# Block sums of batch 0's values from the groups fetched for attention, constants written on chip, and a new order of instructions

## The chip, the cores and the metric

The kernel runs on one core of a Trainium2 chip, in one launch. The metric is the device time of one execution in microseconds (us). The core has five instruction streams that run side by side and wait for each other through semaphores: PE (TensorE, matmuls and transposes), ACT (ScalarE), DVE (VectorE), POOL (GpSimd) and SP (SyncE, which here issues all DMAs). Each stream executes its own instructions strictly in order.

## What is computed

Attention with a local window and block summaries feeds a layer that mixes tokens and channels. B = 4 batches, H = 8 heads, S = 768 tokens, D = 64.

```python
k_sum = k.reshape(B, H, nb, 32, D).max(axis=3)        # nb = 24 blocks
v_sum = v.reshape(B, H, nb, 32, D).mean(axis=3)
scores_l = scale * q @ k.T, kept where |pos_q - pos_k| < 16, else -1e9
scores_s = scale * q @ k_sum.T + log(32)
a = softmax(concat([scores_l, scores_s]))
x = a @ concat([v, v_sum])                             # (B, S, 512)
theta = x @ w_theta;  zr, zi = x * cos(theta), x * sin(theta)
y = w_tok_r @ zr + w_tok_i @ zi                        # over tokens
u = x + y
out = u + relu(u @ w_ch)
```

The four weight matrices arrive as 64-bit floats and are turned into 32-bit ones on chip, by integer operations on ACT, POOL and DVE.

## The kernel before

A batch's 768 queries are cut into six tiles of 128, numbered 0 to 23 over the four batches. A tile's 128 rows are two groups of 64 queries, and a group sees 94 local keys (64 and a halo of 15 on either side) beside the 24 block summaries: 118 columns (`NK`), the summaries first. Group j's 96 rows of local values (94, padded to `VL` = 96) come by one DMA from the array `vg` into rows 24 to 119 of a tile `v`; the 24 summed rows are copied into rows 0 to 23. Four such tiles are in rotation.

The steps, with the letters used below and the line of their main instruction:

- **S** scores, 32 matmul records a tile (L465; the first tile's in two halves); softmax of eight heads on DVE (L501) and ACT (L505)
- **P** transposes of the softmax, two halves of four (L514), each copied out of PSUM by ACT or DVE (L518)
- **A** products with the values, 32 records (L488), then the normalisation (L526 to L535)
- **X** transposes of the normalised tile (L544), copied out by ACT or DVE (L294)
- **T** theta, four products over the channels (L569 for tiles 0 to 5, with unsplit 32-bit operands; L574 after that), then the phase (L583 to L587) and cosine and sine (L592 to L599)
- **M** the mix over tokens, per batch, half of the channels and token tile s (L637; the steps of batch 0's first half with unsplit operands)
- at the end, the channel product (L753)

Ahead of a batch stands `prepass`. It loads the keys `kn` (four DMAs of 399 KB for batch 0), takes the block maxima on DVE (L392), and forms the block sums of the values. For batch 0 these sums are matmuls (L398): six token tiles of 128 rows are loaded from `vn` by three DMAs into a tile that later holds `x`, and each is multiplied by a 128 by 24 matrix of zeros and ones (`member`), all six into one PSUM bank. ACT scales the result (`vs`, L421), and copies of it go into the `v` tiles (L443). For the other batches DVE sums tiles from `vT`.

Three constant arrays come from the array `cst`: the zeros and ones (22 KB), three masks of 128 by 118 (177 KB), and the identity used by the transposes (64 KB).

The program is first recorded as a list of steps (`op`), numbered as they are made. A string `ORDER`, found beforehand by a search on a planner's costs, names them in the sequence in which they are issued; a letter behind a number picks the engine (p, a, d, g for PE, ACT, DVE, POOL), else it is the one with the least planned cost. Each engine thus gets its instructions in the order of that string. The planner's costs (`SWITCH`, `c_dve` and so on) act on the kernel only through the string and that choice. One more rule stands in the last loop: where a POOL step and the DVE step just ahead of it in the string are both marked with `BOTH`, the POOL step waits for the DVE step.

Before the scores PE runs five products on zeros (L331), which have no result that is used.

Of the kernel before, what the change touches and what calls it, by code (L numbers as in the profile page):

```python
# [14 lines left out]
ALU = mybir.AluOpType  # L15
# [3 lines left out]
B, H, S, D = 4, 8, 768, 64  # L19
P = 128  # L20
NT = S // P
# [9 lines left out]
NK = NB + NL  # L31
VL = 96
# [23 lines left out]
12 6d 14 0 13 15 4 7 8 28 18 9 10 11 3 16 20 1 22 19 33a 37g 35a 34a 39 38a 17 36a 40 41 49 5 52 56 42 44 43 46 50 54 47 74  # L56
75a 24 2 68 76d 51 45 53 48 55 170a 169a 21 23 25 26 59 57 164 29 31 27d 77 78 79 69d 70d 32d 71 72 30a 171 80 212 86 165
167 215g 216g 168g 58a 60a 172 175 176 179 173 174 178 81a 177 61 180 183 182 181 217 62a 184 187 185 186 65d 63 66 64d 67d
82g 166g 83 73 84 87a 188 190 199 88g 92 93 266 189a 191a 218 219 220 221 200a 192 224 223 270a 222 225 196a 193a 103a 213
214 94 95 89 85 90 226 91 194 227 197 229 230 228 195d 198d 231 233 232 269g 104g 108a 105 106 201 202 203 204 205 206d 207  # L60
234 236 271 245 235a 237a 109g 272 275 110 274 323a 276 279 246a 238 111 280 281 208a 242a 239a 278 285 284 320 268 322 267
96 389 97 98 321 99 100 101 102 107 112 113 114a 119a 282 240 273 283 243 241d 244d 277 287 286 247 248 249 250 251 115g
324g 116 117 252d 253 120g 209 288 325 290 299 300a 301 302 254a 289a 291a 292 326 118 255 121 210 122 211 123 258 303 256
124a 334 336 328 337 327 129a 293a 294 392a 296d 335 329 330 393g 125g 130g 259 304 332 295d 297 341 339 333 338 340 305 331
298a 260 394 342 344 126 131 127 132 128 133 312 134a 139a 343a 306d 307 308a 353 354a 309 345a 395 261 355 313 356 346 357
314 358 135g 140d 136 141 137 142 138 143 144a 149a 310 257 145d 347a 350a 150d 351 151 146 348 349a 352a 147 152 148 153
359 154a 159a 681a 360d 361 403 315 366 368 422 369 155g 160d 156 157 161 158 162 163 362a 423a 363 424 425 426 427 311 262a
# [187 lines left out]
def c_dma(nbytes, run=2048):  # L255
# [700 lines left out]
```

## Time and profile before

| | us |
|---|---|
| median of 3 runs | 454.60 |
| lowest, highest | 454.58, 455.56 |
| the profiled execution's time | 454.5 |
| its span (first to last instruction) | 452.7 |
| PE busy | 440.9 |
| DVE, ACT, POOL busy | 336.2, 271.9, 94.0 |
| moved by DMA | 55.80 MB |

The profile is of one execution. Busy times are the union of an engine's instructions; a matmul's end is modelled, so a stretch of back-to-back matmuls is read best from one start to the next. "Idle before" gives the wait just ahead of an instruction and the instruction that released it. Rows of a timeline merge like instructions that follow each other ("x8").

### The profile page before, as it was taken

The page shows a single profiled execution, that of the slowest core. Times are in us where ns is not written, and L with a number is a line of the kernel's source. Part 1 is how long each engine was busy: PE and PEld are TensorE (multiplying, and loading weights), DVE is VectorE, ACT ScalarE, POOL GpSimd, SP SyncE. Part 2 cuts the span into 40 slices and gives each one's busy share as a digit, 9 for nine tenths or more (in the row PEclk, how much of TensorE's full clock was granted, in tenths as well). Part 3 has the DMA queues.
Part 4 walks back from the last instruction along what each step waited for, and adds up shares of the span by engine and source line. Part 5 has one row for each costly group of instructions (what it writes and reads, how often), then busy time and mean ns, then how long its engine had stood idle before and what let it go on. Part 6 is the DMA issues. An engine that isn't in the chain of part 4 may idle for free.

```text
span 452.7 us, 9375 instructions
## 1 busy us (share of the span) xinstructions
PE 440.9 (97%) x3562; PEld 357.3 (79%) x3562; DVE 336.2 (74%) x930; ACT 271.9 (60%) x595; POOL 94.0 (21%) x98
## 2 busy tenths in 40 slices
PE   8888999999999999999999999999999999999997
PEld 3464655757888888888888888888888878999996
DVE  4799999778576576776638757575654599998996
ACT  2899988887774676966373755366664406526240
POOL 0221204635520103041011100012003100313521
PEclk9999999999999999999999999999999999999999
DMA  8999945323077340412710503101003720000256
GB/s 300 344 332 327 373 154 184 119 60 110 1 227 250 101 119 25 130 42 52 229 37 3 163 1 118 41 3 55 0 2 108 274 85 0 0 19 20 88 186 250
DMA packets 25005, 55.80 MB, mean 123 GB/s; under 512 B 2944, under 2 KB 8320, under 8 KB 24960
## 3 DMA queue, kind: packets, MB, share of 16 engines
q1 hardware_dynamic: 24960, 55.20, 37.4%
q8 instruction: 28, 0.46, 0.4%
q14 instruction: 17, 0.14, 0.1%
HBM read 45.75 MB, written 9.44 MB: 122 GB/s over the span
## 4 chain that ended last, share of the span: by engine, by line
PE 88%; DMA 8%; ACT 2%; DVE 1%; SPq 0%; issue 0%; ACTq 0%
PE m L637 46%; PE t L574 11%; PE c L753 6%; PE m L753 6%; PE pa L488 5%; PE s L465 4%; PE pa L514 4%; PE t L569 3%; DMA wt<-wti 3%; PE t L544 3%; DMA v<-vg 2%; DMA x<-vn 2%; DMA kn<-kT 1%; PE t L753 1%; ACT L598 1%; ACT w L598 0%
## 5 line engine op out<-in xcount | busy, mean ns | idle before, releaser
L637 PE MATMUL m<-wt,zh 128*128 128x512 f32 (+1 forms) x768 | 181.2, 360 | 0.8 <-DVE x L656 0.6
L637 PEld LDWEIGHTS m<-wt,zh 128*128 128x128 f32 x768 | 122.8, 189 | 32.8 <-issue 14.3
L637 PE MATMUL m<-wt,zl 128*128 128x512 f32 x336 | 86.6, 339 | 0.0
L505 ACT ACTIVATE e<-e,st 128x118 f32<-128x118 f32 x192 | 62.9, 388 | 16.3 <-DVE st L501 15.9
L637 PEld LDWEIGHTS m<-wt,zl 128*128 128x128 f32 x336 | 51.2, 188 | 7.4
L501 DVE CUSTOM_DVE_ANT_0 e<-s,cs 128x118 f32<-128x118 f32 x192 | 45.4, 273 | 10.7 <-PE s L465 6.8
L574 PE MATMUL t<-wth,xh 128*128 128x512 f32 x144 | 47.6, 412 | 0.0
L583 ACT ACTIVATE w<-t,bmagic 128x512 f32<-128x512 f32 x24 | 16.5, 688 | 42.2 <-PE t L574 41.3
L448 POOL COPY k<-kn 128x376 f32<-128x376 f32 (+1 forms) x24 | 12.7, 536 | 96.2 <-DVE zl L303 39.8
L488 PEld LDWEIGHTS pa<-v,e 118*64 118x64 f32 x768 | 24.7, 137 | 6.8 <-issue 4.2
L514 PEld LDWEIGHTS pa<-cs,e 128*118 128x118 f32 x192 | 22.7, 136 | 8.9 <-ACT e L505 1.6
L514 PE MATMUL pa<-cs,e 128*118 128x128 f32 x192 | 28.5, 274 | 0.8 <-ACT e L505 0.4
L488 PE MATMUL pa<-v,e 118*64 118x65 f32 x768 | 28.2, 224 | 0.8 <-ACT e L518 0.8
L574 PE MATMUL t<-wth,xl 128*128 128x512 f32 x72 | 28.3, 394 | 0.0
L465 PE MATMUL s<-k,q 64*64 64x118 f32 x768 | 25.3, 268 | 1.3 <-DVE st L527 0.7
L465 PEld LDWEIGHTS s<-k,q 64*64 64x64 f32 x768 | 19.7, 132 | 7.8 <-issue 5.9
L656 DVE TENSOR_TENSOR x<-m,x 128x512 f32<-128x512 f32 (+1 forms) x32 | 16.6, 548 | 11.6 <-PE m L637 11.6
L586 DVE TENSOR_SCALAR w<-w 128x512 f32<-128x512 f32 x19 | 8.6, 451 | 22.4 <-ACT w L583 22.3
L518 DVE COPY e<-pa 118x512 f32<-118x512 f32 x15 | 10.3, 688 | 18.9 <-PE pa L514 18.9
L574 PEld LDWEIGHTS t<-wth,xh 128*128 128x128 f32 x144 | 22.1, 189 | 2.7 <-DVE xl L550 0.3
L303 POOL TENSOR_TENSOR zl<-zb,zh 128x512 fp32r<-128x512 f32 x9 | 11.5, 1289 | 58.6 <-ACT zh L294 31.6
L587 DVE CUSTOM_DVE_ANT_0 w<-t,w 128x512 f32<-128x512 f32 x24 | 16.6, 690 | 8.0 <-POOL w L586 7.4
(168 smaller groups left out, 798.9 us busy)
## 6 DMA issues: line engine op xcount, KB each, us to landing
v<-vg SPq DMA_DIRECT2D x48, 195.0 KB, 4.5
q<-qg SPq DMA_DIRECT2D x24, 256.0 KB, 4.5
kn<-kT SPq DMA_DIRECT2D x6, 798.0 KB, 7.7
wt<-wtr SPq DMA_DIRECT2D x6, 768.0 KB, 10.1
wt<-wti SPq DMA_DIRECT2D x6, 768.0 KB, 11.9
f<-vT SPq DMA_DIRECT2D x12, 384.0 KB, 4.9
cu<-u_scratch SPq DMA_DIRECT2D x8, 384.0 KB, 6.4
out<-cu SPq DMA_DIRECT2D x16, 192.0 KB, 2.5
```

The lines of the kernel that those rows point to most:

```text
L465: mm(0.79 * len(pairs) / NP, [lambda p=p, g=g, h=h: nc.tensor.matmul(sc[h].get()[ROW[g], p], q.get()[ROW[h], p, ROW[g]], k.get()[ROW[h], p ...
L488: mm(2 * 0.433 + scores[0] + (0.2 if scores[0] else 0.0), [lambda n=n, g=g, a=a: nc.tensor.matmul(xa[a].get()[ROW[g], n], turned[a].get()[ ...
L501: op({"DVE": 0.205}, lambda eng, n=n: nc.vector.tensor_tensor_reduce(e()[:, n], sc[n % 2].get()[:, 2 * a + n // 2], mask(m), -SCALE, 3.0e3 ...
L505: op({"ACT": 0.288}, lambda eng, n=n: nc.scalar.activation(e()[:, n], e()[:, n], AF.Exp, bias=st.get()[:, n:n + 1], scale=-1.0), [(st, n)] ...
L514: mm(NH * 0.109, [lambda n=n: nc.tensor.transpose(tp.get()[:NK, n], e()[:, n], ident()) for n in range(NH)], [e_ref, (cs, "ident")], [tp], ...
L544: mm(NC * 0.109, [lambda c=c: nc.tensor.transpose(tx.get()[:, c], xn[b, i].get().rearrange("p h d -> p (h d)")[:, c * P:(c + 1) * P], ident())
L574: calls = [lambda t=t, xx=xx, k=k, c=c: nc.tensor.matmul(th.get(), xx.get()[:, c], w_th[c].get()[:, k], start=(c == 0 and t == 0), stop=(c ...
L583: op({"ACT": 0.59}, lambda e: nc.scalar.activation(r(), th.get(), AF.Identity, bias=bmagic.get(), scale=1.0 / TWO_PI), [th, bmagic], [R], due)
L587: op({"DVE": c_dve(DM)}, lambda e: nc.vector._custom_dve(TENSOR_ADD_SAT, out=r(), in0=th.get(), in1=r(), s0=PI_F, s1=-PI_F), [th], [R], due)
L637: nc.tensor.matmul(acc[th](), zz.get()[:, r, cc], w[:, TT[th]], start=(s == 0 and r == 0 and t == 0 and (th == 0 or c == 0)), stop=(s == N ...
L656: op({"DVE": c_dve(nt * P)}, lambda e, u=u, acc=acc: nc.vector.tensor_tensor(u(), acc(), u(), op=ALU.add), [areg] + [(xs, n) for n in rang ...
L753: calls = [lambda k=k, t=t, x=x, y=y: nc.tensor.matmul(to.get(), weights[n][x][0]()[:, k, j * P:(j + 1) * P], operands[n].get()[:, y, k], ...
```

## The change

**Block sums of batch 0.** The three DMAs from `vn` go. The groups 0 to 7 of batch 0 are fetched in `prepass` (eight DMAs of 195 KB from `vg`, which tiles 0 to 3 need anyway), groups 0 to 3 into the four rotating tiles and groups 4 to 7 side by side in the space of an `x` tile (`wide`). A group's 64 queries cover two blocks of 32, so each group is multiplied by a 96 by 24 matrix of zeros and ones that has two columns of ones (`pair`). The last two token tiles still come from `vn`, 256 KB each. Six products become ten, into the same bank. The tiles 0 to 3 then fetch no values of their own, and there are eight copies of the sums into value tiles instead of four for batch 0.

**Rows.** Local keys come first (rows 0 to 95, two of them padding that the mask removes), the 24 summaries last: 120 columns instead of 118.

**Constants.** The three DMAs from `cst` go. 17 instructions write masks, zeros and ones, and the identity: memsets on DVE and POOL, and `affine_select` on POOL.

**Order.** A new string. Counting the steps as the code makes them, it begins so on each engine (W0 to W3 are the four pieces of `w_theta`, W4, W5, ... those of the token weights; before in brackets where it says more):

- SP: groups 4, 0, 1, 2, keys, group 5, keys, group 3, keys, keys, queries of tile 0, group 6, `vn` 4, group 7, W1, `vn` 5, W0, queries, W3, queries, W2, W4, a group, W5. (Before: keys, keys, zeros and ones, queries, keys, keys, `vn` 0-1, masks, `vn` 2-3, W1, `vn` 4-5, identity, W0, queries, group 0, group 1, W2, queries, W3, group, group, W4, W5.)
- PE: four of the products on zeros, six block-sum products, S0, four block-sum products, P0, S1, A0, the fifth product on zeros, S2, P1, X0, A1, T0, S3, P2, X1, A2, T1, P3, S4, A3, X2, T2, M of s = 0 (four), S5. (Before: five on zeros, S0, six block-sum products, P0, S1, A0, S2, P1, X0, A1, T0, P2, S3, X1, A2, T1, half of P3, S4, half of P3, X2, half of T2, A3, M.)
- POOL: twelve of the constants, in the middle of which the masks, then a copy of key maxima, the identity's second step, key copies.
- ACT, from tile 0's last exponential on: `vs`, W0's first step, two copies of the sums, one half of P0, a copy of the sums, W3's first step, tile 1's exponentials, W2's first step, both halves of P1, X0, a copy of the sums, and tile 2's exponentials mixed with the first steps of W4 and W5 and key copies.
- DVE, from tile 0's softmax on: W1 (five steps), one half of P0, W0's third step, a copy of the sums, W0's fourth, tile 1's softmax, tile 0's normalisation, W3, W0's last, W3, three of tile 2's softmax steps, W3's last, W2's three steps and a step of tile 1's normalisation.

Further on the tiles follow each other as before; where two halves of P stood on either side of a T product, they now mostly stand together. Some 200 steps change between DVE, ACT and POOL. ACT switches between its exponential and sine tables 27 times instead of 23.

```diff
-VL = 96
+LW = NL + 2
+NK = LW + NB
...
-    dma(lambda: sums.get().rearrange("p a n -> p (a n)")[:, :2 * NB - BPT], lambda: cst[:, P + 3 * NK:], (2 * NB - BPT) * 512, [], [sums], 1e6)
-    for k, c in (("mask", slice(P, P + 3 * NK)), ("ident", slice(0, P))):
-        dma(lambda c=c: cs.get()[:, c], lambda c=c: cst[:, c], (c.stop - c.start) * 512, [], [(cs, k)], 1e6)
+    def fill(dst, value, n, wr):
+        op({"DVE": c_dve(n, "fast"), "POOL": c_pool(n, False)}, lambda e: V[e].memset(dst(), value), [], [wr], -100.0, port=BOTH)
+
+    def keep(dst, pattern, n, base, step, compare, value, wr):
+        op({"POOL": c_pool(n, False) + 0.1}, lambda e: nc.gpsimd.affine_select(
+            out=dst(), in_=dst(), pattern=pattern, compare_op=compare, fill=value, base=base, channel_multiplier=step), [], [wr], -100.0, port=BOTH)
...
+    for g in range(2):
+        local = lambda g=g: masks(slice(g * QT, (g + 1) * QT), slice(0, LW))
+        keep(local, [[0, 3], [1, LW]], 3 * LW, 0, -1, ALU.is_ge, far, (cs, "mask"))
+        keep(local, [[0, 3], [-1, LW]], 3 * LW, 2 * HALO, 1, ALU.is_ge, far, (cs, "mask"))
...
-                st = Ref(tpool, [P, NT, DM], tag="x", bufs=K["XB"])
-                for t in range(0, NT, 2):
-                    dma(lambda t=t: st.get()[:, t:t + 2], lambda t=t: vn[b, t:t + 2].rearrange("t p d -> p t d"), 2 * P * DM * 4, [], [(st, t)], due)
-                    mm(2 * 0.93, [product(t, lambda t=t: st.get()[:, t]) for t in (t, t + 1)], [(st, t), sums], [pv], due, mode="block")
+                wide = Ref(tpool, [P, NT * DM], tag="x", bufs=K["XB"])
+                tail = Ref(tpool, [P, DM], tag="zb", bufs=K["ZS"])
+                vbuf[b] = [Ref(apool, [NK, H, DV], tag="v", bufs=K["VB"]) for _ in range(K["VB"])]
...
+                for j, (at, key, _) in enumerate(here):
+                    vload[j] = at, key
+                    loc = (key, "loc") if j < K["VB"] else (wide, (j, "loc"))
+                    dma(lambda at=at: at()[:LW], lambda j=j: vg[b, j], H * (LW + 16) * DV * 4, [], [loc], due, 2080, 0.35)
+                    mm(0.93, [lambda at=at, j=j: nc.tensor.matmul(
+                        pv.get()[:NB].rearrange("n p d -> n (p d)"), flags(pair - 2 * j, pair - 2 * j + NB)[:LW], at()[:LW, :, :D],
+                        start=(j == 0), stop=False)], [loc, sums], [pv], due, mode="block")
+                for t, (at, key) in zip((NT - 2, NT - 1), ends):
+                    dma(at, lambda t=t: vn[b, t], P * DM * 4, [], [key], due)
+                    mm(0.93, [product(t, at)], [key, sums], [pv], due, mode="block")
...
+            if b > 0 or j >= 8:
+                dma(lambda at=at: at()[:LW], lambda j=j: vg[b, j], H * (LW + 16) * DV * 4, [], [keys_v[0]], due, 2080, 0.35)
```

## Rows read from the trace of the kernel before

**Rows 1.** The page: busy time by engine, and GB/s in 40 slices of 11.3 us.

```profile
PE 440.9 (97%) x3562; PEld 357.3 (79%) x3562; DVE 336.2 (74%) x930; ACT 271.9 (60%) x595; POOL 94.0 (21%) x98
GB/s 300 344 332 327 373 154 184 119 60 110 1 227 250 101 119 25 130 42 52 229 37 3 163 1 118 41 3 55 0 2 108 274 85 0 0 19 20 88 186 250
```

**Rows 2.** Busy time by stretches of 5 us: PE, PE's weight loads, DVE, ACT, POOL (with instructions), PE clock, DMA share, GB/s.

```profile
15.00:20.00 5.00, 4.91 (x75) 2.94 (x74) 4.58 (x17) 3.89 (x10) 0.92 (x3) 1.00 1.05 326
...
30.00:35.00 5.00, 4.63 (x77) 3.28 (x75) 4.93 (x17) 4.71 (x14) 0.83 (x1) 1.00 0.99 342
...
45.00:50.00 5.00, 5.00 (x14) 2.64 (x15) 4.92 (x24) 4.97 (x13) 2.08 (x3) 1.00 1.01 355
```

**Rows 3.** The chain of work that ended last, in order of time, its first pieces: start us, us, what.

```profile
6.43 8.30 DMA x<-vn
...
23.77 12.59 DMA wt<-wti
...
44.94 1.49 PE m L637 x4
```

**Rows 4.** The timeline of the first 15 us: start us, us, engine, line, operation, out<-in, count, idle before.

```profile
1.46 7.61 PE L331 MATMUL t<-zb 128*128 128x512 f32 x10 [1.46 <-DVE zb L329]
...
6.75 0.34 PEld L331 LDWEIGHTS t<-zb 128*128 128x128 f32 x1 [0.52 <-issue]
...
7.60 0.22 PEld L331 LDWEIGHTS t<-zb 128*128 128x128 f32 x1 [0.52 <-issue]
...
8.05 0.19 PEld L331 LDWEIGHTS t<-zb 128*128 128x128 f32 x1 [0.24 <-issue]
...
8.98 0.34 POOL L448 COPY k<-kn 128x188 f32<-128x188 f32 x1 [8.53 <-DMA kn<-kT]
...
9.01 0.63 PE L465 MATMUL s<-k,q 64*64 64x118 f32 x16
...
10.81 3.61 PE L398 MATMUL pa<-x,vt 128*24 128x512 f32 x8
```

**Rows 5.** The timeline from 16 to 37 us, the same columns.

```profile
16.70 0.59 ACT L421 ACTIVATE vs<-pa 24x512 f32<-24x512 f32 x1 [0.73 <-PE pa L398]
...
17.32 0.62 ACT L443 COPY v<-vs 24x520 f32<-24x520 f32 x1
17.32 0.42 DVE L443 COPY v<-vs 24x520 f32<-24x520 f32 x1
...
18.04 1.07 ACT L518 COPY e<-pa 118x512 f32<-118x512 f32 x2
18.11 0.69 DVE L361 SCALAR_TENSOR_TENSOR xh<-wth,xh 128x512 int32<-128x512 int32 x1
...
18.89 1.28 PE L488 MATMUL pa<-v,e 118*64 118x65 f32 x31
19.04 0.28 DVE L501 CUSTOM_DVE_ANT_0 e<-s,cs 128x118 f32<-128x118 f32 x1 [0.24 <-PE s L465]
...
20.27 0.64 ACT L353 ACTIVATE xh<-wth 128x512 f32<-128x512 f32 x1
...
20.71 0.16 DVE L527 TENSOR_SCALAR st<-pa 128x4 f32<-128x4 f32 x1
...
21.00 0.61 POOL L357 TENSOR_SCALAR xh<-xh 128x512 f32<-128x512 f32 x1 [0.41 <-ACT xh L353]
...
21.59 0.76 DVE L535 TENSOR_TENSOR xn<-pa,st 128x256 f32<-128x256 f32 x2
...
23.24 0.67 ACT L353 ACTIVATE xl<-wth 128x512 f32<-128x512 f32 x1 [0.75 <-DMA wth<-wth]
...
36.45 0.92 ACT L353 ACTIVATE f<-wt 128x768 f32<-128x768 f32 x1 [0.57 <-DMA wt<-wti]
```

**Rows 6.** PE alone from 24 to 45 us, the same columns.

```profile
24.48 1.46 PE L488 MATMUL pa<-v,e 118*64 118x65 f32 x32 [0.82 <-ACT e L518]
...
29.41 1.04 PE L514 MATMUL pa<-cs,e 128*118 128x128 f32 x8
30.37 1.04 PE L465 MATMUL s<-k,q 64*64 64x118 f32 x32
...
41.88 1.12 PE L569 MATMUL t<-xh,x 128*128 128x512 f32 x2 [1.18 <-ACT x L294]
```

**Rows 7.** PE alone from 206 to 213 us, the same columns; the start-to-start times are what is read.

```profile
206.39 0.86 PE L637 MATMUL m<-wt,zh 128*128 128x512 f32 x4
...
207.52 1.04 PE L465 MATMUL s<-k,q 64*64 64x118 f32 x32
208.49 1.16 PE L488 MATMUL pa<-v,e 118*64 118x65 f32 x32
209.57 0.66 PE L544 MATMUL t<-cs,xn 128*128 128x128 f32 x4
209.99 0.95 PE L637 MATMUL m<-wt,zh 128*128 128x512 f32 x4
...
211.12 0.86 PE L637 MATMUL m<-wt,zh 128*128 128x512 f32 x4
...
212.16 0.86 PE L637 MATMUL m<-wt,zh 128*128 128x512 f32 x4
```

**Rows 8.** Groups of instructions by line: what POOL's dearest form costs (busy us, mean ns of one, idle before).

```profile
L303 POOL TENSOR_TENSOR zl<-zb,zh 128x512 fp32r<-128x512 f32 x9 | 11.5, 1289 | 58.6 <-ACT zh L294 31.6
```

More of the change, by code (lines that the diff above doesn't have):

```diff
@@ L133 @@
+1982 1983 2002 2003 2004
 """
@@ new lines, in attn_moe @@
+    fill(lambda: masks(slice(QT, P), slice(HALO + QT, LW))[:, 2], far, HALO + 2, (cs, "mask"))
+    fill(flags, 1.0, 2 * NB - BPT, sums)
+    keep(flags, [[-BLK, 2 * NB - BPT]], 2 * NB - BPT, BLK * (NB - BPT), 1, ALU.is_ge, 0.0, sums)
+    keep(flags, [[BLK, 2 * NB - BPT]], 2 * NB - BPT, BLK - 1 - BLK * (NB - BPT), -1, ALU.is_ge, 0.0, sums)
+    pair, width = 2 * NB - BPT + NB - 2, 2 * NB - 2
+    fill(lambda: flags(2 * NB - BPT, 2 * NB - BPT + width), 0.0, width, sums)
+    fill(lambda: flags(pair, pair + 2), 1.0, 2, sums)
@@ L438, in att_tile @@
         dma(q.get, lambda: qg[b, i], NP * P * 512, [], [q], due)
-        v = [vbuf[b][(2 * i + g) % K["VB"]] for g in range(2)]
+        v = []
         for g in range(2):
-            dma(lambda g=g: v[g].get()[NB:], lambda g=g: vg[b, 2 * i + g], H * (VL + 16) * DV * 4, [], [(v[g], "loc")], due, 2080, 0.35)
-            if 2 * i + g < K["VB"]:
-                op({"POOL": c_pool(H * DV, False), "ACT": c_act(H * DV), "DVE": c_dve(H * DV, "fast")}, lambda e, g=g: (
-                    nc.scalar.copy if e == "ACT" else V[e].tensor_copy)(v[g].get()[:NB], vs.get()), [vs], [(v[g], "sum")], due, port=BOTH)
+            j = 2 * i + g
+            if b == 0 and K["VB"] <= j < 8:
+                (at, (own, n)) = vload[j]
+                keys_v = [(own, (j, "loc")), (own, (j, "sum"))]
+            else:
+                own = vbuf[b][j % K["VB"]]
+                at, keys_v = own.get, [(own, "loc"), (own, "sum")]
+            v.append((at, keys_v))
+            if b > 0 or j >= 8:
+                dma(lambda at=at: at()[:LW], lambda j=j: vg[b, j], H * (LW + 16) * DV * 4, [], [keys_v[0]], due, 2080, 0.35)
+            if j < (K["VB"] if b else 8):
+                op({"POOL": c_pool(H * DV, False), "ACT": c_act(H * DV), "DVE": c_dve(H * DV, "fast")}, lambda e, at=at: (
+                    nc.scalar.copy if e == "ACT" else V[e].tensor_copy)(at()[LW:NK], vs.get()), [vs], [keys_v[1]], due, port=BOTH)
         k = Ref(apool, [P, NP, 2, NK], tag="k", bufs=K["KB"]) if i < K["KB"] else kbuf[b][i % K["KB"]]
@@ L488, in products @@
         mm(2 * 0.433 + scores[0] + (0.2 if scores[0] else 0.0), [lambda n=n, g=g, a=a: nc.tensor.matmul(
[L489 to L490 removed]
+            xa[a].get()[ROW[g], n], turned[a].get()[:NK, n * P + g * QT:n * P + (g + 1) * QT], v[g][0]()[:NK, NH * a + n], start=True, stop=True)
+            for a in range(2) for n in range(NH) for g in range(2)] + scores[1], v[0][1] + v[1][1] + turned + scores[2], xa + scores[3], due, mode="block")
         for a in range(2):
```

225 lines of the change are left out of this document (112 added, 113 removed).

## The prediction

> **What bounds the kernel now.** I read the page first: PE is busy 440.9 of 452.7 us, every other engine has a quarter of the span or more to spare, and DMA is heavy only in the first 60 us (300 to 373 GB/s in the first five slices) [rows 1]. So the end moves by what is added to or taken from PE's own work, and by PE's waits; DMA, DVE and ACT count only where PE waits for them. The stretches of 5 us show where that is: ahead of 45 us PE has gaps (4.63 of 5 us from 30 to 35) while DMA stands at a share of 1 and DVE at 4.6 to 4.9 of 5 us; from 45 us on PE is full [rows 2]. The chain says the same: up to the first mix step at 44.94 it runs mainly through loads (the values from `vn`, a token weight), and after that through PE [rows 3]. The case is therefore decided in the head, up to M of s = 0; a delay there is carried to the end nearly one to one.
>
> **The start, worked out from the order in the diff.** The products on zeros run in passes: the weight loads, each made one pass ahead, start 0.85 us apart up to 7.60 and 0.45 after it, and the one for pass ten starts with pass nine, at 8.05 [rows 4]. That halving is the step of the clock from 1.2 to 2.4 GHz, though the granted clock is written as 1.00 already. Four of the five products stand first in the new order, so eight passes are over at 8.05 and the first block-sum product can start there, where S0 started at 9.01.
>
> A block-sum product takes two passes: eight records in 3.61 us make 0.45 a pass with the last end counted, and 0.86 a product by passes of 0.43, half the cold 0.85 (these eight are four products) [rows 4]. Ten need 8.6 us where six needed 5.2: 3.4 us more on PE, in order. Six of them stand ahead of S0, so S0 cannot start before 8.05 + 5.2 = 13.25.
>
> Is its data there? SP now issues four groups (780 KB) before the first keys and 2,766 KB up to the last ones; before it was 1,874 KB, landed at about 8.9 (the wait of POOL's first copy ends there) [rows 4]. The third pair of `vn` tiles, at 4,099 KB, landed at 14.73 [rows 3], so 2,225 KB took 5.85 us, 380 KB a us. The last keys come at 8.9 + 892/380 = 11.2, their maximum (1 us) and copies (0.3) make it 12.6: hidden behind the six products, just. The last `vn` tile, at 4,436 KB, lands at 15.6, before its product (17.0) needs it. The fetch of 1.3 MB less (four `vn` tiles and the constants) thus moves nothing in the first 18 us; it lets the weights that wait behind come 0.3 to 3 us earlier.
>
> The constants: POOL has twelve of them ahead of the first product, four of 288 elements. At the rate of its copies (0.34 us for 188) they take 0.45 each and the chain ends near 6 us [rows 4]; at that of its dearest form, 1.29 us for 512 [rows 8], near 7.2. Both are before 8.05, so I take no cost; below nothing it cannot go, since nothing waited for POOL there. Before, the mask's DMA held the first softmax step back; now it waits for S0.
>
> So S0 runs from 13.3 to 14.4, the last four block-sum products to 17.85. ACT then works in order: `vs` 0.59, W0's first step 0.64, two copies 0.62 each, a half of P0 0.54 (two took 1.07) [rows 5]: A0 can start at 21.3, where it started at 18.89 [rows 5], 2.4 late. What queues behind it on PE is S2 and P1. On DVE, W0's third step waits for that ACT step and for POOL's 0.61, then come 0.42, 0.42 and 0.69, and tile 1's softmax starts at 21.8 and ends at 23.5; before it was 19.04 to 20.71 [rows 5], 2.8 late. Normalisation (1.45), P1 (25.2 to 25.9), W2's first step and both halves of P1 on ACT (1.7) bring A1 to 27.35, against 24.48 [rows 6]: 2.9 late. T0's third product needs W2, whose last step on DVE stands behind W3, W0 and three softmax steps: 24.95 + 5.1 = 30.1. T0 ends at 32.0; before it ended at 29.41 [rows 6]. The lag there is 2.6 us, and it contains the 3.4 us of products and 1.0 of the earlier start.
>
> **From T0 to the first mix step.** Before, this took from 29.41 to 44.9, of which PE's work (P2, S3, X1, A2, T1, P3, S4, X2, half of T2, A3 by the starts in rows 6) is 11.8 and waits are 3.7. The new order does the other half of T2 (two products of two passes, 0.86 each) first, so the point to compare with is 46.6. With the same waits M starts at 32.0 + 15.5 + 1.7 = 49.2, a lag of 2.6. With the chain carried on (ACT has four weight steps of 0.92, two copies of keys and a table load among the exponentials, DVE ends tile 3's softmax at 41.2, so P3 starts at 42.4 and T2 at 47.1) it is 50.6, a lag of 4.0. With no wait at all it would be 45.5, 1.1 ahead. The lighter DMA speaks for the lower end, since W3 and a token weight were waited for by 0.75 and 0.57 us [rows 5]; DVE's fill of over 90% speaks for the upper [rows 2]. I take 3.0, between the two counts that have waits.
>
> **From there on.** (1) Changes of kind on PE. A mix step takes 1.04 from start to start, 1.13 after transposes, and 1.13 ahead of scores; A, behind scores, takes 1.08 [rows 7]. After the first mix step the old order has 55 changes from transposes to a wide product and 17 from wide products to scores, the new one 31 and 8: 33 times 0.09 is 3.0 less. It has 14 more changes of other kinds (scores or A next to transposes or to wide products), which rows 6 and 7 bound by 0 and 0.25 (P2 ahead of S3 took 0.96, 0.25 over two halves of 0.36); at 0.14, the middle, that is 2.0 more. Sum: 1.0 less, between 3.0 less and 0.5 more. (2) 120 columns: S takes 0.97 [rows 7]; two columns in 118 over 24 tiles are at most 0.4 us, I take 0.3. The transposes and A have as many moving columns as before; DVE's and ACT's two columns lie beside PE. (3) Five tiles now have both halves of P, then S, then A with nothing between, so both copies out of PSUM (0.54 on ACT [rows 5]) must be done within 0.97. The nearest row is A1, which waited 0.82 with only X0 in between [rows 6]. Bounds 0 and 5 times 0.8; I take 0.2, since S is 0.6 longer than X. (4) POOL takes over work and ACT four more table loads; neither is near full after 100 us, and I take nothing. (5) The waits at X6 and at the prepass of batch 1 have the same neighbours in both orders and stay. The tail after the last product is unchanged.
>
> **Sum.** Against the profiled execution: 454.5 + 3.0 - 1.0 + 0.3 + 0.2 = 457.0. The median of the runs is 454.6, 0.1 above that execution, which changes nothing.
>
> **Rivals.** *The load was the bound, faster.* The chain of the old head is DMA throughout [rows 3]. If what I count as waits for ACT and DVE is shadow of late loads, the 1.3 MB shorten the head: with 1.5 us of waits in place of 7.0 (from S0 at 9.0 to the mix at 44.9 PE had 28.9 of work by the same starts), the new head (34.7 us of PE work from 8.05) ends at 44.3 against 46.6, and with the -1.0 and +0.5 the run takes 451.7. It decides at A0: if A0 starts before 19.5, this holds. Against it stands ACT's fixed order ahead of A0, each step with a row. *Lag and savings cancel.* If T0 ends 2 us late and PE's waits up to the mix fall by 1, the lag is about 1.0, the changes of kind give 1.0 back, the columns and P's copies cost 0.5, and the time is 455.0. *The constants are late.* Everything in the head hangs on POOL's chain, which DVE's memset releases at about 1.5 us; from 8.05 on each us that it ends late is a us more. Were the chain twice as long as by the dearer rate, it would end near 12, and the run takes 461. The trace has no `affine_select`; POOL's first copy took its 0.34 us right behind the load that it waited for [rows 4], so I give this little. The Trainium skill, GPSIMD Engine Reference, section Instruction dispatch, says that the first call of a freshly loaded kernel pays some 6 us of code load that the profile shows as no instruction; by that, as an estimate, the chain would end near 12 to 13. No row here shows such a load.
>
> **How the numbers follow.** About 0.3% of the time, 1.4 us, is what a measurement can tell from no change. Chances: the lag as worked out, 457.0, 0.45 (its own spread of some 2 us puts 0.38 of that over +1.4, 0.06 within, 0.01 below); the load as bound, 451.7, 0.28 (0.25 faster, 0.03 within); cancelling, 455.0, 0.22 (0.04, 0.16, 0.02); late constants, 461, 0.05. Faster 0.30, same 0.25, slower 0.45. The range leaves out the late constants and the lower half of the faster case's spread, and takes in the upper lag with some waits of (3): 451.2 to 460. Its ends stand on different signs; the likeliest case alone has 455 to 459.5.
>
> **What would show it.** The first block-sum product at 8.0 to 8.3 with POOL's last constant before it; S0 near 13.3; A0 near 21, behind ACT's copies and not behind a load; T0's end near 32; the first mix step at 49 to 51, with PE full after it; mix steps after transposes fewer by about twenty. What would make the prediction wrong: a first mix step before 47.5 (the waits of the head shrank), POOL's constants ending after 8 us, or PE gaps of over 2 us in sum after 100 us.

## The result, and the profile after

| | before | after |
|---|---|---|
| time, us (median of 11 runs each, same chip) | 455.22 (453.94 to 457.67) | 458.42 (456.68 to 461.12) |
| profiled execution, us | 454.5 | 458.0 |
| its span, us | 452.7 | 456.3 |

The ratio is 1.0073, with a 95% interval of 1.0055 to 1.0091: 3.3 us slower (2.5 to 4.1), where the forecast was 2.5. Nine of the changed kernel's eleven runs had a mean granted clock of 0.998 or more, with a median of 458.20, so the clock is not what separates the two kernels. The page of the changed kernel, to be held against [rows 1]:

```profile
PE 443.8 (97%) x3570; PEld 358.2 (79%) x3570; DVE 336.6 (74%) x935; ACT 275.2 (60%) x579; POOL 108.0 (24%) x128
GB/s 245 378 344 393 329 11 123 140 30 163 2 168 187 121 165 122 59 1 50 246 59 37 177 26 37 100 36 1 1 2 139 215 108 1 1 0 55 52 192 258
```

PE is 2.9 us busier, ACT 3.3, POOL 14. In its first slice of 11.4 us DMA moved 245 GB/s where it had moved 300. The stretches of 5 us from 5 us on (columns as in [rows 2]) show the same, here of the changed kernel:

```profile
5.00:10.00 5.00, 5.00 (x10) 1.55 (x9) 1.29 (x2) 0.28 (x1) 0.36 (x2) 1.00 1.04 287
10.00:15.00 5.00, 5.00 (x43) 1.59 (x40) 2.88 (x7) 2.14 (x5) 1.71 (x6) 1.00 1.06 340
```

and here of the kernel before:

```profile
5.00:10.00 5.00, 4.64 (x23) 1.83 (x21) 2.88 (x5) 1.29 (x5) 0.34 (x1) 1.00 1.01 370
10.00:15.00 5.00, 4.41 (x25) 1.30 (x26) 2.44 (x20) 3.10 (x10) 0.00 (x0) 1.00 1.05 398
```

DMA is full in all four (its share, the last but one number, is 1.01 to 1.06), and in the changed kernel it moves less. PE's timeline, up to the first mix step:

```profile
8.12 3.61 PE L440 MATMUL pa<-v,vt 96*24 96x512 f32 x8
...
13.44 1.05 PE L516 MATMUL s<-k,q 64*64 64x120 f32 x32
...
18.41 1.40 PE L565 MATMUL pa<-cs,e 128*120 128x128 f32 x8
...
21.51 1.15 PE L539 MATMUL pa<-v,e 120*64 120x65 f32 x32 [0.72 <-ACT e L569]
...
31.52 1.05 PE L516 MATMUL s<-k,q 64*64 64x120 f32 x32
...
44.67 1.13 PE L620 MATMUL t<-xh,x 128*128 128x512 f32 x2 [0.68 <-ACT x L295]
...
48.20 2.31 PE L688 MATMUL m<-wt,zh 128*128 128x512 f32 x6
```

The start came as worked out: first block-sum product 8.12 (8.05), S0 13.44 (13.3), A0 21.51 behind an ACT copy (21.3), T0's end 31.52 (32.0). The first mix step stands at 48.20, 1.6 behind the 46.6 that the kernel before is to be compared with, where I took 3.0.

Both are single executions, and the head differs between executions of the same instructions (more on that with the order, below).

To see the rest, I added up for each step of PE the start-to-start time that it takes where nothing waits (mix 1.04, S 0.97, A 1.09, a half of P or X 0.36, a block-sum product 0.86, and so on): 415.6 us before, 419.0 after, and the difference is the four products. What is left over at each point is waits, gaps and changes of kind:

| PE reaches | before, us | left over, us | after, us | left over, us |
|---|---|---|---|---|
| first mix step | 44.88 | 18.1 | 48.20 | 16.2 |
| S of tile 8 | 97.46 | 22.0 | 100.98 | 21.0 |
| S of tile 14 | 182.32 | 25.8 | 187.38 | 23.9 |
| S of tile 18 | 245.81 | 27.9 | 246.97 | 27.7 |
| last product | 448.18 | 33.6 | 451.52 | 33.5 |

Up to the first mix step the changed kernel has 5.16 us more work, 1.72 of it the half of T2 that now stands first, and it gets there 3.32 us later. So the head does save 1.8 us of waits, and all of it is given back later: the end is 3.34 us late, and the four products are 3.44. That equality is a sum, not a cause; the experiments say what is in it. Two places of the give-back, on PE of the changed kernel: the transposes of tile 15 (X15) and a late mix step. The kernel before has no wait at the first, and one of 0.62 at the second (the last row):

```profile
229.33 0.66 PE L595 MATMUL t<-cs,xn 128*128 128x128 f32 x4 [1.21 <-DVE w L638]
...
368.72 0.98 PE L688 MATMUL m<-wt,zh 128*128 128x512 f32 x4 [1.21 <-DVE x L707]
```

```profile
365.56 0.73 PE L637 MATMUL m<-wt,zh 128*128 128x256 f32 x3 [0.62 <-DVE x L656]
```

### The profile page after: what moved, and what is told of

Read it like the earlier page. It is cut to its first block, busy times and chain, and to the rows that moved or that the text cites. A ratio compares the mean times of both kernels' runs of the same rounds, so it can differ in the third digit from the quotient of the medians.

```text
span 456.3 us, 9421 instructions
## 1 busy us (share of the span) xinstructions
PE 443.8 (97%) x3570; PEld 358.2 (79%) x3570; DVE 336.6 (74%) x935; ACT 275.2 (60%) x579; POOL 108.0 (24%) x128
## 4 chain that ended last, share of the span: by engine, by line
PE 77%; issue 7%; ACT 6%; DVE 5%; DMA 3%; POOL 1%; SPq 0%; ACTq 0%; DVEq 0%; POOLq 0%
PE m L688 39%; PE t L625 9%; PE c L804 6%; PE m L804 5%; PE pa L539 4%; PE s L516 4%; PE pa L565 3%; DMA x<-vg 3%; PE t L595 2%; ACT e L556 2%; PE t L620 2%; ACT f L382 1%; DVE wt L393 1%; DVE f L390 1%; PE t L804 1%
## 5 line engine op out<-in xcount | busy, mean ns | idle before, releaser
L556 ACT ACTIVATE e<-e,st 128x120 f32<-128x120 f32 x192 | 62.7, 388 | 13.1 <-DVE st L552 12.7
L552 DVE CUSTOM_DVE_ANT_0 e<-s,cs 128x120 f32<-128x120 f32 x192 | 44.9, 274 | 4.2 <-PE s L516 1.7
L565 PEld LDWEIGHTS pa<-cs,e 128*120 128x120 f32 x192 | 21.8, 137 | 6.6 <-ACT e L556 2.8
L565 PE MATMUL pa<-cs,e 128*120 128x128 f32 x192 | 26.0, 274 | 1.0 <-ACT e L556 0.4
L539 PEld LDWEIGHTS pa<-v,e 120*64 120x64 f32 x704 | 22.3, 137 | 5.2 <-issue 3.0
L539 PE MATMUL pa<-v,e 120*64 120x65 f32 x704 | 25.4, 224 | 0.7 <-ACT e L569 0.7
L516 PE MATMUL s<-k,q 64*64 64x120 f32 x768 | 25.3, 269 | 0.3 <-issue 0.3
L707 DVE TENSOR_TENSOR x<-m,x 128x256 f32<-128x256 f32 (+1 forms) x32 | 16.5, 550 | 10.2 <-PE m L688 10.2
L569 ACT COPY e<-pa 120x512 f32<-120x512 f32 x30 | 17.0, 588 | 10.5 <-PE pa L565 10.4
L295 ACT CAST wt<-cb 128x768 fp32r<-128x768 f32 x15 | 12.3, 841 | 15.7 <-POOL cb L729 9.1
```

The costliest lines, as they stand in the source:

```text
L516: mm(0.79 * len(pairs) / NP, [lambda p=p, g=g, h=h: nc.tensor.matmul(sc[h].get()[ROW[g], p], q.get()[ROW[h], p, ROW[g]], k.get()[ROW[h], p ...
L539: mm(2 * 0.433 + scores[0] + (0.2 if scores[0] else 0.0), [lambda n=n, g=g, a=a: nc.tensor.matmul(xa[a].get()[ROW[g], n], turned[a].get()[ ...
L552: op({"DVE": 0.205}, lambda eng, n=n: nc.vector.tensor_tensor_reduce(e()[:, n], sc[n % 2].get()[:, 2 * a + n // 2], mask(m), -SCALE, 3.0e3 ...
L556: op({"ACT": 0.288}, lambda eng, n=n: nc.scalar.activation(e()[:, n], e()[:, n], AF.Exp, bias=st.get()[:, n:n + 1], scale=-1.0), [(st, n)] ...
L565: mm(NH * 0.109, [lambda n=n: nc.tensor.transpose(tp.get()[:NK, n], e()[:, n], ident()) for n in range(NH)], [e_ref, (cs, "ident")], [tp], ...
L569: lambda e: (nc.scalar.copy if e == "ACT" else nc.vector.tensor_copy)(t.get()[:NK], tp.get()[:NK].rearrange("k n q -> k (n q)")), [tp], [t ...
```

## The experiments

Each ran beside the kernel before on its chip. Differences are ratio less one, times 455.

**The products taken out, by place.** The late ones:

```diff
-                        start=(j == 0), stop=False)], [loc, sums], [pv], due, mode="block")
+                        start=(j == 0), stop=(j == 5))][:j < 6], [loc, sums], [pv], due, mode="block")
...
-                    mm(0.93, [product(t, at)], [key, sums], [pv], due, mode="block")
+                    mm(0.93, [], [key, sums], [pv], due, mode="block")
```

> The changed kernel without the four block-sum products that stand behind S0 (groups 6 and 7, tiles 4 and 5 of vn); their loads stay. The block sums of batch 0 then cover only the first 386 values or so, so the output differs in that part. PE and load theory: these products cost 3.44 us of PE and wait for loads that land at 15.5 and 17.3 us; without them the copy of the block sums starts at about 14.6 instead of 18.4, A0 near 17.7 instead of 21.5, and the run is 3.0 to 3.9 us shorter than the changed kernel, 454.5 to 455.4, the time of the kernel before. Order theory (the new order of the rest costs the 3 us, and PE's first 20 us are slack): under 1 us shorter, about 458. Constants theory: no change, 458.4.

The early ones:

```diff
-                        start=(j == 0), stop=False)], [loc, sums], [pv], due, mode="block")
+                        start=(j == 4), stop=False)][:j > 3], [loc, sums], [pv], due, mode="block")
```

> The changed kernel without the four products of groups 0 to 3, which stand ahead of S0; their loads stay. The block sums then lack the first 256 values or so, and the output differs in that part. PE work alone (each 0.86 us in the in-order queue counts wherever it stands): 3.4 us shorter, 455.0. Loads set the end of the block sums (the last group lands at 15.5, the last tile of vn at 17.3): S0 moves at most to its keys, 12.6, A0 stays within 0.5 us of 21.5, and the time is 457.9 to 458.4. The two together, with the run without the late products, say whether the work or the landing holds the head.

Measured: 1.0053 (1.0024 to 1.0081) without the late ones, 1.0120 (1.0090 to 1.0150) without the early ones: 3.4 us of PE's work gone, and the first kernel is 0.9 faster than the changed one, within its interval, the second 2 slower. Both PE theories fell: the first run came where the order theory had put it, the second is outside both of its expectations. PE of the kernel without the late products, and stretches of it (columns as in [rows 2]):

```profile
14.21 1.05 PE L516 MATMUL s<-k,q 64*64 64x120 f32 x32 [0.39 <-POOL k L499]
18.36 1.69 PE L565 MATMUL pa<-cs,e 128*120 128x128 f32 x8 [3.10 <-ACT e L556]
```

```profile
15.00:20.00 5.00, 1.79 (x20) 0.96 (x11) 3.90 (x22) 3.90 (x11) 0.55 (x2) 0.94 1.03 387
20.00:25.00 5.00, 4.71 (x80) 3.56 (x83) 4.68 (x26) 4.90 (x12) 2.47 (x5) 0.72 0.88 342
```

P0 waits for an exponential until 4.15 us behind S0's start. In the changed kernel that would be 17.6, and its late products end at 18.4: by these rows all but 0.8 of their 3.4 us lie in the shadow of tile 0's softmax. PE, idle for 3.1 us, was granted 0.72 of its clock in the stretch from 20 us (the last but two number). Without the early products PE was busy for 0.60 of the 5 us from 10, and the granted clock was 0.74, 0.50 and 0.73 in the stretches from 10, 15 and 20 us. These two runs thus mix less work with a slower clock. The next one keeps PE busy:

```diff
+                    if j > 5:
+                        mm(0.93, [zeros], [idle], [bank], due, mode="block")
+                        continue
```

> The changed kernel with the four products behind S0 replaced by products on zeros of the same shape into another bank: PE stays as busy, but the copy of the block sums no longer waits for the loads of groups 6 and 7 and of tiles 4 and 5, nor for these products. The block sums lack that part, and the output differs. If that wait sets A0: the copy moves from 18.4 to 14.6 and A0 from 21.5 to between 18.9 and 19.5, the run 2 to 2.6 us shorter, 456. If the softmax of tile 0, behind S0 at 13.4, sets the head (in the run without these products PE waited for an exponential until 18.4): P0 stays at 18.4, A0 moves by under 1 us, and the time is 457.6 to 458.4.

Measured 1.0061 (1.0042 to 1.0080), 2.8 us, 0.5 better than the changed kernel and within the interval. Its PE, at S0 and A0:

```profile
14.55 1.05 PE L521 MATMUL s<-k,q 64*64 64x120 f32 x32 [0.61 <-POOL k L504]
...
22.76 1.15 PE L544 MATMUL pa<-v,e 120*64 120x65 f32 x32 [0.60 <-ACT e L574]
```

The block sums were complete at 14, and S0 started 1.1 later than in the profile of the changed kernel, A0 1.25 later. From S0 to A0 it is 8.2 us, against 8.1 in the changed kernel and in the run without the late products: A0 follows S0 and not the end of the block sums. (This profiled execution took 461.47 against a median of 458.24; its excess lies far behind the head, where PE waited 1.86 us ahead of X15 and the granted clock then fell.) S0 first, then:

```diff
-42 20d 21 22 23 24 34 36 38 26 44 28 40 32 30 56 46 50 48 100 52 94 190 8d 9 0d 15g 1g 2 3 4 5 6g 7g 10 11d 12g 13 14 19 27
+26 28 32 30 56 42 20d 21 22 23 24 34 36 38 44 40 46 50 48 100 52 94 190 8d 9 0d 15g 1g 2 3 4 5 6g 7g 10 11d 12g 13 14 19 16
```

> The changed kernel with the keys and the first queries loaded ahead of the groups, and S0 ahead of all block-sum products, as in the kernel before; the rest in its order. S0 moves from 13.4 to about 9, the block sums end at about 19. If S0's place is what the head pays for (tile 0's softmax behind it): P0 can start at 19 at once and the head is 0.5 to 1.5 us shorter, 456.9 to 457.9. If the ten products set it wherever they stand: A0 stays at 21.3 to 22, and the time is 458.0 to 459.0.

Measured 1.0134 (1.0109 to 1.0160), 6.1 us, outside both expectations. PE of this kernel, and its stretches (columns as in [rows 2]):

```profile
10.00 1.05 PE L515 MATMUL s<-k,q 64*64 64x120 f32 x32 [2.34 <-DMA q<-qg]
11.64 6.92 PE L439 MATMUL pa<-v,vt 96*24 96x512 f32 x8 [0.59 <-DVE st L551]
18.40 3.60 PE L439 MATMUL pa<-x,vt 96*24 96x512 f32 x8
```

```profile
10.00:15.00 5.00, 4.41 (x36) 1.46 (x37) 1.72 (x17) 3.02 (x9) 0.66 (x3) 0.65 1.07 259
15.00:20.00 5.00, 5.00 (x9) 1.06 (x8) 1.52 (x4) 0.00 (x0) 0.00 (x0) 0.66 1.03 344
```

Behind an idle stretch of 2.34 us the first four products ran at half their rate (6.92 us for eight records, then 3.60), which by itself is 3.3 us; the granted clock was 0.65 and 0.66 in these two stretches, where the changed kernel had 1.00. So this median doesn't say what S0's place is worth; it says that where the early block-sum products stood, PE kept its 2.4 GHz. One of the six runs had a granted clock of 1.00: it took 458.95, no less than the changed kernel, but it is one run.

**Parts of the change put into the kernel before.** Constants alone:

```diff
-    dma(lambda: sums.get().rearrange("p a n -> p (a n)")[:, :2 * NB - BPT], lambda: cst[:, P + 3 * NK:], (2 * NB - BPT) * 512, [], [sums], 1e6)
...
+    op({"POOL": 5.0}, constants, [], [sums, (cs, "mask"), (cs, "ident")], -100.0, port=BOTH)
```

> The kernel before, in its own order, with its three constants made on POOL (fills and selections, in place of three DMAs with 270 KB), nothing else changed. If constants on the chip cost nothing (POOL's chain ends near 5 us, ahead of S0 at 9): 0 to 1 us shorter than the kernel before, 454.2 to 455.2, the gain from the first softmax step that no longer waits for the mask's load. Constants theory (they are what makes the changed kernel slower): 2 to 3 us longer, 457 to 458.

Measured 0.9997 (0.9976 to 1.0019): no difference that could be told. In the changed kernel POOL's four 288-element selections took 1.94 us together, and its last constant ahead of the first product ended at 5.43. The products alone:

```diff
-for t in (t, t + 1)], [(st, t), sums], [pv]
+for t in (t,) * (5 if t == 4 else 1) + (t + 1,)], [(st, t), sums], [pv]
```

> The kernel before with four more block-sum products, on tile 4 of vn again, behind the last load of the block sums (tile 4 then counts five times in the block sums, and the output differs in that part). This is the price of 3.44 us of PE work at the end of the block sums in the old order, with the old loads. PE work counts fully: 3.4 us longer, 458.6. Hidden behind loads and the chain on DVE and ACT: 0 to 1 us longer, 455.2 to 456.2. My sum by the head's steps, with some of the delay absorbed by waits up to the first mix step: 2.5 to 3.4 longer, 457.7 to 458.6.

Measured 1.0037 (1.0018 to 1.0057), 1.7 us (0.8 to 2.6), less than my sum had by the head's steps and more than hidden products: P0 moved by 3.2, the first mix step by 2.1 (44.88 to 46.97), since some waits shrank. The loads alone:

```diff
+                    if t < 4:
+                        op({"SP": 0.0}, lambda e: None, [], [], due)
+                        mm(2 * 0.93, [product(t, idle.get) for t in (t, t + 1)], [idle, sums], [pv], due, mode="block")
+                        continue
```

> The kernel before without the loads of tiles 0 to 3 of vn (1.05 MB); their four products run on zeros in the same places. The block sums lack that part, and the output differs. The price of the loads alone, in the old order with the old products. Load theory (the old head waits on loads all the way): the last pair of vn lands 2.8 us earlier and so does everything up to the first mix step, 2 to 3 us shorter, 452.3 to 453.3. If ACT's and DVE's order sets the head: 0 to 1 us shorter, 454.3 to 455.3.

Measured 0.9952 (0.9924 to 0.9981), 2.2 us shorter (0.9 to 3.5). The load theory holds for the old head: 1.05 MB there are worth about 2 us. Part of the size is the clock: of the seventeen runs of the kernel before beside it, eight had a mean granted clock of 0.992 to 0.996, of its own twelve one, and without these the medians are 1.5 us apart. Its profiled execution (454.7, against a median of 452.9) isn't typical of it, and I read no place from it; which waits shrank is therefore not shown.

**The order.** The new order behind the first mix step, in the old program; the old one behind the first mix step in the changed program; the old one behind tile 14's scores in the changed program. The order strings are cut there and spliced; the first steps behind the cut, in the three:

```diff
-258 303 256 124a 334 336 328 337 327 129a 293a 294 392a 296d 335 329 330 393g 125g 130g 259 304 332 295d
+391 390 329 303 304 296a 293d 256 124a 129a 334 297 294 335 328 337 295d 327 336 392a 339 331 305 393a
...
```

```diff
-285 418 366 368 161g 367a 369a 332a 333 166d 162 167 163 168 164 169 334 338 370 377 339 336 378a 379
+418 366 368 336 367a 332a 377 378a 333 369a 419 285 379 337 380 370 381 338 382 161g 166d 162 167 163
...
```

```diff
-956 937a 938 958a 901 974 977 939d 976 975 982 983 985 980 987 979 986 989 984 941 988 978 959d 981
+974 976 977 982 983 975 901 965 1109 966 1110 1021 1022 1023 970 1138 969 1066 985 941 937d 938 939d 956
...
```

> The kernel before (its loads, its constants, 118 columns) with its own order up to the first mix step, and behind it the operations in the order of the changed kernel. By my forecast's terms (changes of kind 1.0 less, copies of P 0.2): 0.8 us shorter, 454.4 to 455.0. Tail theory: 1.5 to 2.0 us longer, 456.8 to 457.3. Head theory, with the order as good as the old one: 455.2 to 455.8.

> The changed kernel with its own order up to the first mix step, and behind it the operations in the order of the kernel before (engines too). Head theory (the loss is made ahead of the first mix step, by the ten block-sum products and what they push back, and is carried to the end): no gain, 458.0 to 459.5; by my forecast's term for the changes of kind the old order would even cost 1.0 more, 459.4. Tail theory (1.6 us are lost ahead of the first mix step and about 1.7 by the new order behind it): 456.3 to 457.0.

> The changed kernel with its own order up to the scores of tile 14 (187 us in its trace), and behind them the order of the kernel before. Aligned with the kernel before, the changed kernel loses 1.8 us of waits and gaps between tile 14 and the last product (9.6 us against 7.8), in two places above all: 1.4 us ahead of X15 and 0.5 us more in the mix of the last step. If those are the new order's doing there: 1.5 to 1.8 us shorter than the changed kernel, 456.6 to 456.9. If they are backlog that DVE and ACT carry from the head and any order meets (as with the old order from the first mix step on, which gained 0.3): 458.0 to 458.6.

Measured 1.0047 (1.0025 to 1.0068), 1.0063 (1.0044 to 1.0082) and 1.0091 (1.0063 to 1.0119). The new order costs the old program 2.1 us, as tail theory had it, but the old one gives the changed program nothing back: 2.9 and 4.1 us against 3.3. What is left over from the first mix step to the last product: 15.6 before, 17.3 after, 17.0 for the new order in the old program, 17.1 and 16.8 for the old order in the changed one. That looks as if each order fitted its own program, but the traces divide it otherwise. When the scores of tile 9 start, PE has the same matmuls left in all of these kernels. PE at that point and at the start of the last product, of the kernel before, of the changed one, of the new order in the old program and of the old order behind the first mix step in the changed one:

```profile
108.97 1.04 PE L465 MATMUL s<-k,q 64*64 64x118 f32 x32
...
448.18 0.33 PE L753 MATMUL m<-wt,xh 128*128 128x384 f32 x1
```

```profile
110.94 1.05 PE L516 MATMUL s<-k,q 64*64 64x120 f32 x32
...
451.52 0.33 PE L804 MATMUL m<-wt,xh 128*128 128x384 f32 x1
```

```profile
109.64 1.04 PE L464 MATMUL s<-k,q 64*64 64x118 f32 x32
...
450.22 0.33 PE L752 MATMUL m<-wt,xh 128*128 128x384 f32 x1
```

```profile
113.31 1.05 PE L515 MATMUL s<-k,q 64*64 64x120 f32 x32
...
452.40 0.33 PE L803 MATMUL m<-wt,xh 128*128 128x384 f32 x1
```

That is 339.21 us before and 340.58 after, 340.58 with the new order in the old program and 339.09 with the old order in the changed one. Over all the profiles the old order takes 339.1 to 339.6 us there, the new one 339.3 to 340.6, and 342.9 in the one execution in which the clock fell behind X15. So this stretch goes with the order and not with the program, and in the new order it costs 0 to 1.4 us, 1.4 in the profile of the changed kernel. The mix step's wait is 1.20 or 1.21 in every profile with the new order there and 0.62 in every other; the wait at X15 differs between executions, from none to 1.86. The old order in the changed program gains this stretch back and loses as much at its seam: from the first mix step to tile 9's scores it takes 63.99 us, the changed kernel 62.74 for the same matmuls. No run has the old order from tile 9 on without such a loss.

The last two kernels' heads are the changed kernel's own, instruction for instruction, and show how it scatters; PE of the third (first mix step at 50.76; 49.32 in the second):

```profile
7.05 2.75 PE L439 MATMUL pa<-v,vt 96*24 96x512 f32 x6
11.44 1.19 PE L439 MATMUL pa<-v,vt 96*24 96x512 f32 x2 [1.64 <-DMA v<-vg]
12.43 3.47 PE L439 MATMUL pa<-x,vt 96*24 96x512 f32 x4
15.82 1.05 PE L515 MATMUL s<-k,q 64*64 64x120 f32 x32
```

PE begins 1.1 us earlier, waits 1.6 for a group, and does four records at half rate (3.47 for 1.88): S0 comes at 15.82 in place of 13.44; the granted clock was 0.72 from 10 to 15 us. In the second it waits 0.8 for that group and 0.6 for the queries, and S0 comes at 14.26. The old head scatters too: with the same instructions up to there the new order in the old program reaches its first mix step at 47.19, where the kernel before has 44.88. So the whole program went into the old order, keys first:

```diff
-42 20d 21 22 23 24 34 36 38 26 44 28 40 32 30 56 46 50 48 100 52 94 190 8d 9 0d 15g 1g 2 3 4 5 6g 7g 10 11d 12g 13 14 19 27
+26 20d 8d 9 0d 15g 1g 2 3 4 5 6g 7g 10 11d 12g 13 14 16 28 27 29 18 21 22 56 32 23 24 25 17 30 34 36 38 40 42 44 46 48 33 59a
```

> The changed program (block sums from the groups, constants on the chip, 120 columns, 1.3 MB less to load) in the order of the kernel before throughout: keys and queries loaded first, S0 ahead of the block sums, then ten products, and the old order from there on; the four copies of the block sums that only the changed program has stand on POOL. From the runs so far, each against the kernel before: four more products in the old order 1.7 us longer, 1.05 MB less to load 2.2 shorter, constants on the chip 0. If these add and the new order is the rest of the loss (it cost 2.1 by itself): 0.5 us shorter to 0.5 longer than the kernel before, 455.0 to 456.0. If ten products on loads by groups lose their time whatever the order (the groups move at 287 to 340 GB/s, not at the 380 that I took): 2.5 to 3.5 us longer, 457.8 to 458.8.

Measured 1.0109 (1.0085 to 1.0133), 5.0 us: outside both expectations. The new order is worth 1.6 us to the changed program, with intervals that just meet. In the traces that is a balance: this kernel reaches the scores of tile 9 at 113.88, 2.9 later than the changed one, and needs 1.2 less from there on. The parts as I had them (1.7 of products, 2.2 less of loads) leave 5.5 us unexplained. In this trace DMA is full and slow while it fetches the groups, 280 GB/s where the kernel before moved 398:

```profile
5.00:10.00 5.00, 4.14 (x23) 1.66 (x21) 2.47 (x5) 1.13 (x4) 0.94 (x4) 1.00 0.97 303
10.00:15.00 5.00, 4.14 (x25) 1.39 (x26) 1.93 (x16) 1.63 (x5) 0.00 (x0) 1.00 1.07 280
```

And there is a part of the change that my forecast had not priced, four more copies of the block sums, for tiles 2 and 3. The last run adds them to the four products, in the old program:

```diff
-            if 2 * i + g < K["VB"]:
+            if 2 * i + g < (8 if b == 0 else K["VB"]):
```

> The kernel before with the four more products of the earlier run (tile 4 of vn counted five times, so the output differs) and with four more copies of the block sums for tiles 2 and 3 on POOL, in the places that they have in the changed program put in the old order. Loads, constants and columns are the old ones. The changed program in the old order was 4.9 us longer than the kernel before, four more products alone 1.7. If the copies (0.61 us each, POOL shares its port with DVE, which is full there) carry the rest: 4.0 to 5.0 us longer, 459.3 to 460.3. If the copies cost nothing: 1.3 to 2.1 longer, 456.6 to 457.4, and the rest lies in the loads by groups. Between: each has a share.

Measured 1.0071 (1.0046 to 1.0096), 3.2 us, between the two: the copies cost 1.5, though the intervals of the two runs overlap (0.8 to 2.6 and 2.1 to 4.4). How, DVE, POOL and PE show; with the products alone first, then with the copies:

```profile
27.90 0.43 DVE L359 TENSOR_SCALAR xl<-xl 128x512 int32<-128x512 int32 x1
28.24 0.68 DVE L364 SCALAR_TENSOR_TENSOR xh<-wth,xh 128x512 uint32<-128x512 uint32 x1
...
31.81 0.56 DVE L359 TENSOR_SCALAR f<-f 128x768 int32<-128x768 int32 x1
32.41 0.96 DVE L361 SCALAR_TENSOR_TENSOR f<-wt,f 128x768 int32<-128x768 int32 x1
...
34.48 0.66 PE L544 MATMUL t<-cs,xn 128*128 128x128 f32 x4 [0.92 <-DVE w L587]
```

```profile
27.98 1.36 POOL L442 COPY v<-vs 24x520 f32<-24x520 f32 x2
28.06 0.81 DVE L358 TENSOR_SCALAR xl<-xl 128x512 int32<-128x512 int32 x1
28.79 1.10 DVE L363 SCALAR_TENSOR_TENSOR xh<-wth,xh 128x512 uint32<-128x512 uint32 x1
...
32.69 1.50 POOL L442 COPY v<-vs 24x520 f32<-24x520 f32 x2
32.77 0.94 DVE L358 TENSOR_SCALAR f<-f 128x768 int32<-128x768 int32 x1
33.75 1.25 DVE L360 SCALAR_TENSOR_TENSOR f<-wt,f 128x768 int32<-128x768 int32 x1
...
36.12 0.66 PE L543 MATMUL t<-cs,xn 128*128 128x128 f32 x4 [1.59 <-DVE w L586]
```

Four DVE steps beside POOL's copies take 0.38, 0.42, 0.38 and 0.29 longer, 1.47 in sum, and X2 starts 1.64 later, the first mix step 1.65 (48.62 against 46.97). POOL itself is idle enough, but DVE, full there, pays.

## Why the forecast came out right, and where its steps were off

The direction and the likeliest case held: the head ends late, and the lag reaches the end. That the size came so near is in part luck. In the profiled execution the head's lag was 1.6 where I had 3.0, and the stretch behind it added 1.7 where I had 0.5 less: two errors of opposite sign. And one of my own signs of being wrong came: PE gaps of over 2 us in sum after 100 us. The two waits shown above make 2.42, where the kernel before has 0.62 there. Point by point:

- **The start.** Right to 0.2 us up to A0, in the profiled execution. The count of the queue was wrong: I had it at 380 KB a us, the last keys at 11.2 and everything "hidden behind the six products, just". POOL's copy behind the last keys started at 12.35 here, at 13.18 and 14.08 in the two runs with the same head, where S0 came at 14.26, behind a wait for queries, and at 15.82, behind products that had waited for a group. The first mix step stood at 48.2, 49.3 and 50.8: lags of 1.6, 2.7 and 4.2 against the 46.6, which itself is one execution's. The 3.0 lies in the middle of these, the profiled execution at their short end; a part of the size came from loads that I had called hidden.
- **The fetch of 1.3 MB less, which was to move nothing in the first 18 us.** For the old head that was wrong: 1.05 MB are worth about 2 us there. For the changed order no run tests it. The change doesn't show that gain, and up to 15 us it moves 3.9 MB (161, 287 and 340 GB/s in the three stretches) where the old one moved 4.8 (198, 370 and 398); that the slower loads eat the gain is argued from these rows, not shown by a run.
- **Changes of kind, 1.0 less.** This step was too large. From the first mix step to the last product, left over less the waits above 0.3 us, the gaps are 12.6 before (15.6 less 3.0), 12.6 with the new order in the old program (17.0 less 4.4) and 12.1 after (17.3 less 5.2): 0 to 0.5 less. With slightly other times for the steps the same count gives 0.3 to 0.8 less, so it is good to some 0.3 us.
- **Waits behind the first mix step, 0.2 more.** This step failed by most: 5.2 against 3.0, 2.2 more (4.1 against 1.7, 2.4 more, by the idle times that the rows themselves show). I had counted the five pairs of P and taken "nothing" for the 200 steps that change engine. The longest new ones are the mix step's and X15's, shown above. At X15 the phase of a theta tile goes from ACT (0.69) over POOL (0.62) to DVE (0.69) late, and X waits for DVE to empty the bank.
- **Four copies of the sums.** They had a place in the list of steps and no term in the sum. In the old order they cost 1.5 us. In the new one two stand on ACT (0.62 each, where ACT has no gap over 0.2 us from 18.5 to 42) and two on POOL; what they cost there was not measured.
- **120 columns, 0.3.** In the old order the stretch from tile 9's scores to tile 23's has 7.7 left over with 118 columns and four more products, 7.8 with 120: 0.1 for fourteen tiles.
- **The rivals.** *Load as bound* (A0 before 19.5) did not occur, though its premise was true of the old head. *Late constants* fell, in both programs: the last one ahead of the first product ended at 5.43. *Cancelling* was right about the waits in the head and wrong that nothing else comes.

In the old order the account is 1.7 (products), 1.5 (copies) and 1.8 more for the rest of the program, each uncertain by about 1; the new order takes 1.6 off. In the traces the rest is 1.2, and 0.8 of it has a place. Between the scores of tile 7 and those of tile 8 the old order takes 9.83 us with four more products, 9.84 in the kernel before and with the copies, but 10.65 in the changed program (10.64 behind the first mix step). A DVE step and a POOL step that make low parts of weights run side by side there; DVE and POOL with four more products first, then of the changed program in the old order, with PE's wait behind them:

```profile
93.50 0.94 DVE L303 TENSOR_TENSOR wt<-wt 128x768 fp32r<-128x768 f32 x1
93.26 2.32 POOL L303 TENSOR_TENSOR wth<-xl,wth 128x512 fp32r<-128x512 f32 x1
```

```profile
95.86 1.92 DVE L303 TENSOR_TENSOR wt<-wt 128x768 fp32r<-128x768 f32 x1
95.62 1.34 POOL L303 TENSOR_TENSOR wth<-xl,wth 128x512 fp32r<-128x512 f32 x1
...
99.55 1.06 PE L564 MATMUL pa<-cs,e 128*120 128x128 f32 x8 [0.47 <-ACT e L555]
```

In the old program POOL's step is the one that is stretched, in the changed one DVE's, and a softmax on DVE comes late by it. Why the two change places is open, and so are the other 0.4 us, in which the loads by groups may be. No version tried beats the kernel before, apart from the one that leaves loads out.

## What to carry to other kernels

Price a saved load by the stretch in which it is saved and by the rate of what is put in its place, and price every small copy that a shared buffer brings with it, by what runs beside it and not by its engine's spare time. Splice two orders before you blame one, and compare the spliced kernels where the same work is left: a seam can cost what the better stretch behind it gains. Taking work out of PE's idle time went with a slower clock in two runs here, so put work on zeros in its place when you test it.

## What the hardware showed that I had not expected

- POOL copies of 24 by 520 stretched DVE steps beside them from 0.43 to 0.81, 0.68 to 1.10, 0.56 to 0.94 and 0.96 to 1.25 us, and a pair of copies took 1.36 and 1.50 us where one by itself takes 0.61. The Trainium skill, SBUF — State Buffer, section Terms, calls the port pair of the two engines an exclusive lock for a whole instruction. These rows agree in part: the four DVE steps grow by 1.47 where they overlap the copies by about 2.7. The rows of the two low-part steps agree better: the step that lost grew by 0.98, on either engine, where the two overlap by about 1.
- PE idle for 1.64 to 3.10 us was followed by a granted clock of 0.65 to 0.72 in a stretch of 5 us in several executions (1.64 and 0.72, 1.86 and 0.66, 2.34 and 0.65, 3.10 and 0.72), and by products at half rate (6.92 us against 3.61). But it isn't the idle time alone: in the run with less to load PE was idle for 2.53 us, the granted clock stayed at 1.00, and the eight records behind took their 3.61:

```profile
11.96 0.63 PE L469 MATMUL s<-k,q 64*64 64x118 f32 x16 [2.53 <-ACT k L452]
12.52 3.61 PE L398 MATMUL pa<-zb,vt 128*24 128x512 f32 x8
```

- Loads of groups: 287 and 340 GB/s from 5 to 15 us in the changed kernel, 303 and 280 with its program in the old order, at a DMA share of 0.97 to 1.07, where keys and value tiles had 370 and 398.
- The same instructions reach the first block-sum product at 7.05, 7.22, 7.33, 7.46 or 8.12 us in different executions.
